# Attention and mixture-of-experts kernel: earlier value requests, other PSUM banks for two transposes, a last tile in halves

## The chip, the cores and the metric

The kernel runs on one core of a Trainium2 chip. The metric is the device time of one execution in microseconds; lower is better. Six executions of the kernel before took 402.0 to 403.68 us, with a median of 403.0 us.

## The reference

The first half is attention: 4 batches, 8 heads, 768 positions, 64 elements for each head. Heads 0, 2 and 6 ("retrieval") see every earlier key; the other five ("streaming") see the first 4 keys and a window of 64. The second half sends the 3072 rows of 512 elements through four experts, each with two layers, and adds their outputs with given weights:

```python
mask = np.where(retr[0, :, 0, 0, None, None], full_mask, stream_mask)
scores = np.where(mask[None, :, :, :], scale * q @ k.T, -1000000000.0)
a = softmax(scores); attn_out = a @ v
x = attn_out.transpose(0, 2, 1, 3).reshape(B * S, H * D)
p = domain_probs / (domain_probs.sum(-1, keepdims=True) + 1e-09)
for e in range(E):                       # E = 4
    h = np.maximum(x @ w1[e], 0.0)       # 512 -> 1024
    out += p[:, e:e + 1] * (h @ w2[e])   # 1024 -> 512
```

## The kernel before

**Groups.** The 3072 rows are cut into G = 8 groups of 384 (half a batch each). For a group, `attention` makes xT, the group's attention output transposed: four column tiles ct of 128 rows, each holding two heads. `moe_group` then runs the four experts over it. Groups overlap: while TensorE (PE) does the experts of group g, single steps of the attention of group g + 1 are put between its matmuls, by a written budget of time (`tick`, `att_ns`). Only group 0 has nothing to run beside: its attention comes first, alone. The order on every engine is the order in which the program is written; nothing is rescheduled.

**Group 0's attention** (`first`). Queries and keys of batch 0 come as float32 through the queues of SP and ACT, and TensorE transposes them (L495). For each head, `scores` multiplies (L596, L608), ACT takes the exponential into es (L614), and `values` multiplies es by the values: L644 for retrieval heads (tiles vR), L708 for streaming heads (tiles vS). Retrieval heads are divided on DVE (L657, L661, L664) into x_pair or x_one, which TensorE transposes (L685) and DVE copies to xT (L689). Streaming heads get a logarithm and an exponential on ACT (L726, L736) and a product on DVE (L731). Here and there `warm_up` (L387) puts matmuls on zeros between them, whose results nobody reads. The order at the end is: scores of head 7 together with values of head 6, values of head 5, the transposes of heads 2 and 6, values of head 7.

**Requests on POOL.** The values of all heads, the weights (converted to float16 on the way) and all later inputs are requested by POOL, one after another, in one queue (L268 and L274 values, L299 first-layer weights w1sb in two halves per expert, L305 second-layer weights w2sb). At the start the order is: values of head 0, the masks, values of heads 2, 1, 3, 4, then w1 of expert 0, values of heads 5, 6, 7, w2 of expert 0, clearing of tiles, keys and queries of group 1 (L211), w1 of expert 1, some of group 1's values, w2 of expert 1, and so on.

**Group 1's attention** still uses TensorE for the transposes of queries and keys (L498), four pairs hp of heads, queries and keys apart; DVE copies the results out: L507 queries, L514 and L530 keys (kS at L530). From group 2 on, DMA does these transposes.

**PSUM.** There are three pools: pA with four banks (`bank()`: scores, transposes of q and k, first layer of the experts), pV with two (values), pO with two (second layer, some values).

**The experts.** For each expert, the first layer makes eight tiles of 4 matmuls of 384 columns (L850, 32 in all), each read out by ACT (L863). The second layer makes three output tiles of 128 rows x 512 columns (L871, 8 matmuls each), which DVE scales and adds to acc (L883 for the first expert, L887 after). With the last expert, SP requests the store of each tile (L892).

Of the kernel before, what the change touches and what calls it, by code (L numbers as in the profile page):

```python
# [9 lines left out]
FP32 = mybir.dt.float32  # L10
FP16 = mybir.dt.float16
AF = mybir.ActivationFunctionType
ALU = mybir.AluOpType
# [4 lines left out]
def kernel(  # L18
# [33 lines left out]
    nc = tc.nc  # L52
    P = 128
    B, H, S, D = q.shape
    E, DM, F = moe_w1.shape
# [6 lines left out]
    FTP = F // P  # L62
    NTILE = N // P
    G = B * NCH
# [24 lines left out]
    pV = ctx.enter_context(tc.tile_pool(name="pV", bufs=1, space=bass.MemoryType.PSUM))  # L89
# [8 lines left out]
    def bank():  # L98
        return pA.tile([P, 512], FP32, name="pA", bufs=4)
# [3 lines left out]
    w2sb = pers.tile([P, E * FTP, DM], FP16, name="w2sb")  # L103
# [32 lines left out]
    p_sb = pers.tile([P, NTILE, E], FP32, name="p_sb")  # L136
# [19 lines left out]
    def own_v(h):  # L156
        return half(PLACE[h][1])
# [10 lines left out]
    def v_tiles(b, c, h):  # L168

        if RETR[h]:  # L170
            return vR[b % 2][:, 3 * c : 3 * c + 3, RH.index(h), :]
        if b:
            return windows(vSf, c)[:, :, SH.index(h), :]
        return vS[:, c, :, SH.index(h), :]
# [10 lines left out]
    def rows_of(x, b, h, c):  # L185
        return x[b, h, c * CH : (c + 1) * CH, :].rearrange("(j p) d -> p j d", p=P)

    def tiles_of(x, b, h, c):
        return x[b, h, c * CH : (c + 1) * CH, :].rearrange("(t r) d -> r t d", r=TK)

    def windows_of(x, b, h, c):

        assert b > 0
        first = ((b * H + h) * S + c * CH - WO) * D
        return bass.AP(x.tensor, x.offset + first, [[D, P], [WQ * D, WT], [1, D]])
# [68 lines left out]
    def load_v(b, c, heads):  # L264
        for h in heads:
            t = v_tiles(b, c, h)
            if RETR[h]:
                gp.dma_start(out=t[:, :, 0:D], in_=rows_of(v, b, h, c))  # L268
            elif b:
                gp.dma_start(  # L270
                    out=t[:, :, own_v(h)], in_=windows_of(v, b, h, c)
                )
            else:
                gp.dma_start(  # L274
                    out=t[R0:P, :, own_v(h)],
                    in_=tiles_of(v, b, h, c),
                )
# [72 lines left out]
    for h in range(H):  # L350
        if h == 2:
            nc.sync.dma_start(
                out=v_s32, in_=v[0, :, 0:NS, :].rearrange("h r d -> r h d")
            )
        nc.sync.dma_start(out=k32[:, :, h, :], in_=rows_of(k, 0, h, 0))
        if h == HP:
# [3 lines left out]
                    name=nc.get_next_instruction_name(),  # L360
# [6 lines left out]
        eng = nc.scalar if h < HP else nc.sync  # L367
        eng.dma_start(out=q32[:, :, h, :], in_=rows_of(q, 0, h, 0))
    nc.sync.dma_start(
        out=probs, in_=moe_domain_probs.rearrange("(t p) e -> p t e", p=P)  # L370
# [73 lines left out]

    mask_c(bC, 0.0, -60000.0)
    mask_s(bS[:, 0:2, :], 2, 0.0, -60000.0)
    load_v(0, 0, [2, 1, 3, 4])
    load_w1(0, 0, F)
    load_v(0, 0, [5, 6, 7])
    load_w2(0)  # L450
    zero(gp, kR[0][:, 1, :, :, :])
    zero(gp, kS[:, 1, :, :, :].rearrange("p t s x -> p s t x"))
# [24 lines left out]
    def mm_ns(cols):  # L477
        return cols / 2.4 + 2.5

    def attention(b, c):  # L480
        g = b * NCH + c
        i = b % 2
        first = g == 0
# [4 lines left out]

        def transposes(hp):
            for x, is_k in ((q32 if first else qt16, 0), (k32 if first else k16, 1)):  # L490
                ps = bank()
                for j in range(3):
                    o = ps[:, j * P : (j + 1) * P]
                    if first:
                        nc.tensor.transpose(o, x[:, j, 2 * hp : 2 * hp + 2, :], ident32)  # L495
                        continue
                    for u in range(2):
                        nc.tensor.matmul(  # L498
                            out=o[u * D : (u + 1) * D, :],
                            lhsT=x[:, 2 * hp + u, j, :],  # L500
                            rhs=ident16,
                            start=True,
                            stop=True,
                        )
                if not is_k:
                    op = nc.scalar.copy if first and hp < 2 else nc.vector.tensor_copy
                    op(out=rows_in_order(qTs[b, c][:, hp, :]), in_=cols(ps))  # L507
                    yield t_ns
                    continue
                for u in range(2):  # L510
                    h = 2 * hp + u
                    r = slice(u * D, (u + 1) * D)
                    if RETR[h]:
                        nc.vector.tensor_copy(  # L514
                            out=rows_in_order(
                                kR[i][r, c, RH.index(h), :, :].rearrange(
                                    "r t x -> r (t x)"
                                )
                            ),
                            in_=cols(ps[r, :]),  # L520
                        )
                        continue
                    n = SH.index(h)
                    x_in, x_out = ps[r, 0:CH], kS[r, c, :, n, R0:P]
                    if first:
                        x_in = x_in.rearrange("r (t x) -> r t x", x=TK)
                    else:
                        x_in = x_in.rearrange("r (j t p) -> r j t p", j=3, t=TC)
                        x_out = x_out.rearrange("r t (p j) -> r j t p", j=3)
                    nc.vector.tensor_copy(out=x_out, in_=x_in)  # L530
                    sinks = kS[r, c, :, n, 0:NS]
                    if c == 0:
                        src = ps[r, 0:NS]
                        op = nc.scalar.copy if hp < 2 else nc.vector.tensor_copy
                    else:
                        src, op = kS[r, 0, 0, n, 0:NS], nc.scalar.copy
                    src = src.rearrange("r (o x) -> r o x", o=1)
                    op(out=sinks, in_=src.to_broadcast([D, TC, NS]))
                yield 2 * t_ns
# [288 lines left out]
    def tick(ns):  # L828
        clock[0] += ns
        while behind and behind[0][0] <= clock[0]:  # L830
            behind.pop(0)[1]()


    def moe_group(g):
        nt0 = g * 3
        acc = {}
        for e in range(E):
            hs = moe.tile([P, FTP, CH], FP16, name="hs", tag="hs", bufs=2)


            ahead = 4 if g == 0 and e == 0 else 1
            for f0 in [0, *range(ahead, FTP)]:
                pss = {ft: bank() for ft in range(f0, f0 + (1 if f0 else ahead))}


                cts = (0, 2, 1, 3) if g == 0 else (2, 1, 3, 0)

                def layer1(ft, n):
                    ct = cts[n]
                    nc.tensor.matmul(  # L850
                        out=pss[ft][:, 0:CH],
                        lhsT=w1sb[:, e * DMP + ct, ft * P : (ft + 1) * P],
                        rhs=xT[g][:, ct, :],
                        start=(n == 0),
                        stop=(n == DMP - 1),
                    )

                for ft in pss:
                    for ct in range(DMP - 1):
                        layer1(ft, ct)  # L860
                for ft, ps in pss.items():
                    layer1(ft, DMP - 1)
                    nc.scalar.activation(  # L863
                        out=hs[:, ft, :], in_=ps[:, 0:CH], func=AF.Relu
                    )
                    yield DMP * mm_ns(CH), 0.6
            for j in range(3):
                nt = nt0 + j
                ps_o = pO.tile([P, DM], FP32, name="pO", bufs=2)
                for ft in range(FTP):  # L870
                    nc.tensor.matmul(  # L871
                        out=ps_o,
                        lhsT=hs[:, ft, j * P : (j + 1) * P],
                        rhs=w2sb[:, e * FTP + ft, :],
                        start=(ft == 0),
                        stop=(ft == FTP - 1),
                    )
                    if ft == FTP // 2 - 1:
                        yield FTP // 2 * mm_ns(DM), 1.4
                p_ap = p_sb[:, nt, e : e + 1]  # L880
                if e == 0:
                    acc[nt] = moe.tile([P, DM], FP32, name="acc", bufs=6)
                    nc.vector.tensor_scalar(  # L883
                        out=acc[nt], in0=ps_o, scalar1=p_ap, scalar2=None, op0=ALU.mult
                    )
                else:
                    nc.vector.scalar_tensor_tensor(  # L887
                        out=acc[nt], in0=ps_o, scalar=p_ap, in1=acc[nt],
                        op0=ALU.mult, op1=ALU.add,
                    )  # L890
                if e == E - 1:
                    nc.sync.dma_start(out=out[nt * P : (nt + 1) * P, :], in_=acc[nt])  # L892
                yield FTP // 2 * mm_ns(DM), 1.4
# [87 lines left out]
```

## Time and profile before

| | us |
|---|---|
| median of six runs (lowest, highest) | 403.0 (402.0, 403.68) |
| the profiled execution: its own time | 402.46 |
| the profiled execution: span, first to last instruction | 400.6 |
| TensorE busy | 391.2 (98% of the span) |
| ACT, DVE, POOL busy | 219.3, 155.9, 142.1 |
| attention of group 0, to the first matmul of L850 | 24.2 |
| from there to the last matmul | 372.4 |
| from the last matmul to the end of the span | 4.0 |

The 1.9 us between the span and the execution's own time lie outside the first and last instruction. Line numbers (L850) are those of the kernel before. In the timeline, a row is: start and length in us, engine, line, operation, output and inputs, shape, number of instructions, and in brackets the idle time of the engine before it and what ended that idle time. The rows of matmuls are modelled at their ends: a row's length holds about 0.17 us of the last matmul's way through the array.

### The profile page before, as it was taken

To read this page: it belongs to the slowest core of one execution; us is meant where nothing else is said; L and a number is where in the kernel's file an instruction comes from. 1 tells how busy PE (TensorE), PEld (TensorE's weight loads), DVE (VectorE), ACT (ScalarE), POOL (GpSimd) and SP (SyncE) were. 2 spreads that over 40 slices of the span, in tenths; PEclk is the share of its full clock that TensorE was granted. 3 is DMA by queue.
4 is the path that set the end of the run, shared out by engine and by line. 5 is a ranking of instruction groups with operands and counts; after the bars stand their busy time and mean duration, and the time that the engine had idled before them with its cause. 6 is when DMAs were issued, how large, how long until landed. Compare 5 with 4: busy or idle time off the path is not lost.

```text
span 400.6 us, 7112 instructions
## 1 busy us (share of the span) xinstructions
PE 391.2 (98%) x2821; PEld 222.1 (55%) x2821; DVE 155.9 (39%) x343; ACT 219.3 (55%) x468; POOL 142.1 (35%) x179
## 2 busy tenths in 40 slices
PE   8799999999999999999999999999999999999996
PEld 4664556555555555555555555555555555655552
DVE  7745556424342334334342233433443223422222
ACT  3752668535775545655664446845464456853331
POOL 8943776708908704910039301950000000000000
PEclk9989999999999999999999999999999999999999
DMA  9999999999999969990679949990482000020002
GB/s 168 158 201 200 199 203 153 127 181 134 127 190 147 119 121 119 131 114 2 118 99 161 89 77 136 100 163 12 71 128 81 3 11 0 11 79 2 0 2 79
DMA packets 165989, 42.23 MB, mean 105 GB/s; under 512 B 156380, under 2 KB 160836, under 8 KB 165956
## 3 DMA queue, kind: packets, MB, share of 16 engines
q0 software_dynamic: 102656, 20.98, 61.1%
q1 hardware_dynamic: 61700, 20.40, 26.1%
q10 hardware_dynamic: 1600, 0.39, 0.5%
q8 instruction: 22, 0.36, 0.4%
q14 instruction: 11, 0.09, 0.1%
HBM read 43.57 MB, written 6.29 MB: 124 GB/s over the span
## 4 chain that ended last, share of the span: by engine, by line
PE 90%; POOL 2%; DMA 2%; DVE 2%; ACT 2%; issue 1%; POOLq 0%; ACTq 0%
PE pA L850 41%; PE pO L871 40%; PE pA L596 5%; DMA vR<-in_v_dram 2%; PE pV L644 2%; PE pV L708 2%; PE pO L387 1%; POOL vS L274 1%; ACT es L614 1%; ACT hs L863 1%; DVE kS L530 1%; DVE acc L887 1%; POOL vR L268 0%; POOL bS L411 0%; POOL w1sb L299 0%
## 5 line engine op out<-in xcount | busy, mean ns | idle before, releaser
L850 PE MATMUL pA<-xT,w1sb 128*128 128x384 f16 x1024 | 185.9, 326 | 0.9 <-DVE kS L530 0.4
L871 PE MATMUL pO<-w2sb,hs 128*128 128x512 f16 x768 | 181.3, 379 | 0.0
L863 ACT ACTIVATE hs<-pA 128x384 f16<-128x384 f32 x256 | 122.0, 492 | 96.6 <-PE pA L850 91.3
L850 PEld LDWEIGHTS <-w1sb 128*128 128x128 f16 x1024 | 95.9, 98 | 60.4 <-issue 0.8
L871 PEld LDWEIGHTS <-hs 128*128 128x128 f16 x768 | 71.6, 98 | 73.2 <-ACT hs L863 0.7
L614 ACT ACTIVATE es<-pA 128x384 f16<-128x384 f32 (+2 forms) x122 | 60.6, 510 | 52.9 <-PE pA L596 50.4
L887 DVE SCALAR_TENSOR_TENSOR acc<-pO,p_sb,acc 128x512 f32<-128x512 f32 x72 | 54.0, 750 | 72.3 <-PE pO L871 72.0
L226 POOL DMA_DIRECT2D kSr<-in_k_dram x30 | 29.9, 1001 | 33.6 <-DMA kS<-kSr 22.5
L222 POOL DMA_DIRECT2D kRr<-in_k_dram x18 | 14.0, 778 | 73.0 <-DMA kR<-kRr 71.1
L731 DVE TENSOR_TENSOR xT<-pV,rc 64x384 f16<-64x384 f32 x37 | 20.5, 553 | 30.9 <-ACT rc L736 20.7
L270 POOL DMA_DIRECT2D vS<-in_v_dram x30 | 30.4, 1027 | 0.5 <-DMA q<-in_q_dram 0.5
L618 DVE TENSOR_TENSOR es<-es,mC 128x256 f16<-128x256 f16 (+1 forms) x42 | 10.9, 259 | 48.1 <-ACT es L614 47.2
L883 DVE TENSOR_SCALAR acc<-pO,p_sb 128x512 f32<-128x512 f32 x24 | 18.0, 751 | 27.9 <-PE pO L871 27.7
L726 ACT ACTIVATE rc<-pV,eps 64x384 f32<-64x384 f32 x37 | 21.3, 575 | 13.1 <-PE pV L708 12.5
L596 PE MATMUL pA<-qT,kR 128*128 128x384 f16 (+2 forms) x120 | 24.8, 278 | 0.7 <-ACT qT L507 0.4
L736 ACT ACTIVATE rc<-rc 64x384 f32<-64x384 f32 x38 | 19.8, 521 | 1.2
L268 POOL DMA_DIRECT2D vR<-in_v_dram x24 | 19.4, 809 | 1.8 <-DMA q<-in_q_dram 1.6
L644 PEld LDWEIGHTS <-es 128*128 128x128 f16 x252 | 13.3, 97 | 9.3 <-issue 2.1
L644 PE MATMUL pV<-vR,es 128*128 128x65 f16 x252 | 15.6, 193 | 2.1 <-DMA vR<-in_v_dram 1.9
L708 PEld LDWEIGHTS <-vS 128*128 128x128 f16 x255 | 13.8, 98 | 6.8 <-issue 0.5
L618 DVE TENSOR_TENSOR es<-es,mW 128x384 f16<-128x384 f16 x30 | 10.7, 358 | 17.1 <-ACT es L614 17.1
L596 PEld LDWEIGHTS <-kR 128*128 128x128 f16 x120 | 11.3, 98 | 10.2 <-DVE kR L514 0.7
(91 smaller groups left out, 185.1 us busy)
## 6 DMA issues: line engine op xcount, KB each, us to landing
out_dram<-acc SPq DMA_DIRECT2D x24, 256.0 KB
w1sb<-in_moe_w_dram POOLq DMA_DIRECT2D x8, 512.0 KB, 13.0
w2sb<-in_moe_w_dram POOLq DMA_DIRECT2D x4, 1024.0 KB, 15.5
kSr<-in_k_dram POOLq DMA_DIRECT2D x30, 112.0 KB, 3.9
vS<-in_v_dram POOLq DMA_DIRECT2D x30, 112.0 KB, 5.5
q<-in_q_dram POOLq DMA_DIRECT2D x18, 128.0 KB, 4.4
vR<-in_v_dram POOLq DMA_DIRECT2D x24, 48.0 KB, 4.6
kRr<-in_k_dram POOLq DMA_DIRECT2D x18, 48.0 KB, 4.2
```

The costliest lines, as they stand in the source:

```text
L226: gp.dma_start(out=kSr[:, :, SH.index(h), own(h)], in_=windows_of(k, b, h, c),)
L270: gp.dma_start(out=t[:, :, own_v(h)], in_=windows_of(v, b, h, c))
L596: nc.tensor.matmul(out=ps[:, o : o + nq], lhsT=key_tile(b, c, h, t), rhs=qTs[b, c][:, hp, q0 : q0 + nq], start=(n == 0 or not first), stop ...
L614: nc.scalar.activation(out=es[:, 0:cols], in_=ps[:, 0:cols], func=AF.Exp, scale=SC)
L618: nc.vector.tensor_tensor(out=es[:, o0:o1], in0=es[:, o0:o1], in1=m[:, mo : mo + o1 - o0], op=ALU.mult,)
L644: nc.tensor.matmul(out=ps[:, j, 0 : D + 1], lhsT=lhsT, rhs=vR[i][:, t, RH.index(h), 0 : D + 1], start=(n == 0), stop=(n == len(work) - 1), ...
L708: nc.tensor.matmul(out=ps[:, q0 : q0 + nq], lhsT=v_tile(b, c, h, t), rhs=es[:, o : o + nq], start=(n == 0), stop=(n == len(work) - 1), ski ...
L726: nc.scalar.activation(out=rc[r, :], in_=ps[o, 0:CH], func=AF.Ln, bias=eps[o, :])
L850: nc.tensor.matmul(out=pss[ft][:, 0:CH], lhsT=w1sb[:, e * DMP + ct, ft * P : (ft + 1) * P], rhs=xT[g][:, ct, :], start=(n == 0), stop=(n = ...
L863: nc.scalar.activation(out=hs[:, ft, :], in_=ps[:, 0:CH], func=AF.Relu)
L871: nc.tensor.matmul(out=ps_o, lhsT=hs[:, ft, j * P : (j + 1) * P], rhs=w2sb[:, e * FTP + ft, :], start=(ft == 0), stop=(ft == FTP - 1),)
L887: nc.vector.scalar_tensor_tensor(out=acc[nt], in0=ps_o, scalar=p_ap, in1=acc[nt], op0=ALU.mult, op1=ALU.add,)
```

## The change

There are three edits.

1. POOL's requests at the start: values of heads 6, 5 and 7 are requested directly after those of heads 2, 1, 3 and 4, and w1 of expert 0 after all of them. Before, w1 of expert 0 came first, and heads 5, 6, 7 after it. w2 of expert 0 follows in both.
2. In group 1, the transposes of the first two pairs of heads (four tiles: queries and keys of hp 0 and 1) take the two banks of pV in turn; those of hp 2 and 3 take banks of pA as before. Group 0 is not changed.
3. The last output tile of all (group 7, expert 3, third tile) is made by a new function `last_tile`: two halves of 256 columns, one after the other, each with 8 matmuls in a bank of pV, its own step on DVE, and its own store; the first is requested by SP, the second by ACT.

Nothing else moves: on each engine the other instructions stand in the same order.

```diff
-    load_v(0, 0, [2, 1, 3, 4])
+    load_v(0, 0, [2, 1, 3, 4, 6, 5, 7])
     load_w1(0, 0, F)
-    load_v(0, 0, [5, 6, 7])
     load_w2(0)
...
-                ps = bank()
+                if first or hp > 1:
+                    ps = bank()
+                else:
+                    ps = pV.tile([P, 512], FP32, name="pV", bufs=2)
...
+    def last_tile(e, nt, hs, acc):
+        for n, eng in enumerate((nc.sync, nc.scalar)):
+            cols = slice(n * DM // 2, (n + 1) * DM // 2)
+            ps = pV.tile([P, 512], FP32, name="pV", bufs=2)
+            for ft in range(FTP):
+                nc.tensor.matmul(
+                    out=ps[:, 0 : DM // 2],
+                    lhsT=hs[:, ft, 2 * P : 3 * P],
+                    rhs=w2sb[:, e * FTP + ft, cols],
+                    start=(ft == 0),
+                    stop=(ft == FTP - 1),
+                )
+            nc.vector.scalar_tensor_tensor(
+                out=acc[:, cols], in0=ps[:, 0 : DM // 2],
+                scalar=p_sb[:, nt, e : e + 1], in1=acc[:, cols],
+                op0=ALU.mult, op1=ALU.add,
+            )
+            eng.dma_start(out=out[nt * P : (nt + 1) * P, cols], in_=acc[:, cols])
...
+                if g == G - 1 and e == E - 1 and j == 2:
+                    last_tile(e, nt, hs, acc[nt])
+                    continue
```

## The prediction

> **What bounds the kernel now.** I read the page's chain that ended last, then the timeline of TensorE over the first 45 us and of all engines over the last ten, then POOL's timeline and the DMA view, because the first edit moves requests.
>
> ```profile
> span 400.6 us, 7112 instructions
> ...
> PE 90%; POOL 2%; DMA 2%; DVE 2%; ACT 2%; issue 1%; POOLq 0%; ACTq 0%
> ```
>
> TensorE is the chain, so only what makes it wait, slow down or end later counts. Its timeline shows where:
>
> ```profile
> 16.74 1.04 PE L387 MATMUL pV<-warm 128*128 128x256 f16 x8
> 19.72 0.34 PE L644 MATMUL pV<-vR,es 128*128 128x65 f16 x6 [1.94 <-DMA vR<-in_v_dram]
> 22.09 2.01 PE L387 MATMUL pO<-warm 128*128 128x256 f16 x10
> 24.19 5.64 PE L850 MATMUL pA<-xT,w1sb 128*128 128x384 f16 x32
> 35.62 1.47 PE L850 MATMUL pA<-xT,w1sb 128*128 128x384 f16 x8
> 37.78 2.12 PE L850 MATMUL pA<-xT,w1sb 128*128 128x384 f16 x12 [0.40 <-DVE kS L530]
> 42.09 1.03 PE L871 MATMUL pO<-w2sb,hs 128*128 128x512 f16 x4
> ```
>
> Edit 1 aims at the 1.94 us before 19.72 (head 6's values), edit 2 at the 0.40 us before 37.78, where a first-layer matmul needs a bank that DVE still copies from. The ten warm-ups at 22.09 take 0.2 us each, the eight at 16.74 0.11. The stretches say why (start:end, length, busy time of PE, PEld, DVE, ACT, POOL, then granted clock, DMA share, GB/s):
>
> ```profile
> 16.80:20.21 3.42, 1.47 (x19) 1.21 (x18) 1.23 (x3) 2.01 (x5) 3.42 (x6) 1.00 1.49 186
> 20.21:23.63 3.41, 3.41 (x22) 2.66 (x21) 1.58 (x5) 1.48 (x3) 2.54 (x4) 0.50 1.25 209
> ```
>
> After a stretch with TensorE busy 1.47 of 3.42 us, the clock was 0.50 for 3.41 us: the wait cost 1.94 us and then about 1.7.
>
> **Edit 1 on TensorE.** Six requests change places, none is added. Head 6's request starts at about 9.6, where w1 stood, not at 11.47. Head 4's values, directly ahead, landed at 14.7 (issue 8.92 + 5.8 in the DMA view), and w1's first half, ten times one head's bytes, at 16.7 (9.58 + 7.1). So head 6 lands between 14.7 and 16.7, nearer the former; TensorE asks at 17.6. That wait goes. What is late next:
>
> ```profile
> 18.17 0.69 ACT L614 ACTIVATE es<-pA 128x256 f16<-128x256 f32 x2
> 18.88 0.56 DVE L731 TENSOR_TENSOR xT<-pO,rc 64x384 f16<-64x384 f32 x1
> ```
>
> Head 6's third matmul needs the first of these exponentials, done at about 18.5; ACT has no gap from 15.2 on, so TensorE waits 0.9 us there. Then the transposes at L685 need x_pair: DVE ends L731 at 19.44, and L657, L661, L664 (0.16, 0.17, 0.36) bring it to 20.2, a second wait of about 0.4. From there at full clock: transposes 0.17, ten warm-ups 1.1, four matmuls of head 7 0.25. L850 begins at about 21.8 in place of 24.19: 2.4 us earlier. w1 of expert 0 now stands behind three value requests, but all four had landed by 20.0 (12.21 + 7.8), and the bytes are the same.
>
> **What comes of the 2.4 us.** Expert 1's first layer would begin at 35.62 - 2.4 = 33.2. Its weights are not there. In the DMA view, the request of its second half (issued at 19.71) and POOL's row that waits for its end:
>
> ```profile
> w1sb<-in_moe_w_dram POOLq DMA_DIRECT2D x1, 512.0 KB, 15.4
> ```
> ```profile
> 35.40 0.61 POOL L299 DMA_DIRECT2D w1sb<-in_moe_w_dram  x1 [1.65 <-DMA w1sb<-in_moe_w_dram]
> ```
>
> 19.71 + 15.4 = 35.1. From 20 to 35 us the DMA engines move 202 GB/s without a pause, and the edit changes the order at the head of the queue, not its bytes; POOL's requests from w2 of expert 0 (12.92) on keep their times, because the first that could wait for a displaced transfer starts at 20.3, after 20.0. So L850 starts at 35.16: **-0.46 us** stays of 2.4, and TensorE waits 2.0 us in a new place. Behind that wait stand only TensorE's own matmuls; the query and key transposes of pair 0 are ahead of it. SP's L292 copies, which waited for the values until 20.12, go earlier and have no hurry.
>
> **Edit 2.** From 35.62 to 42.09 there are 6.47 us, 0.40 of them the wait for DVE. L530 ended at 37.73; 2.4 us earlier is 35.3, before the second tile of L850 is done, so the wait would go by edit 1 alone, and with edit 2 the bank is not pA's anyway: **-0.40**, once. Price of the new banks: the queries of pair 1 need pair 0's copied out (L507 ended 35.27, now near 32.9), its keys L530; both are over before their transposes come. The next user of pV, values at 45.7, comes over 3 us after the last of these copies (41.85). Zero, and where DVE is late, 0.4 at most. The next weights: w2 of expert 1 lands at 21.81 + 19.1 = 40.9, TensorE comes at 42.09 - 0.86 = 41.2. Just clear. w1 of expert 2 (35.40 + 12.5 = 47.9) is needed at 49.3. From there on no DMA row ends a wait of TensorE, so the gain reaches the end.
>
> **Edit 3.** The end now:
>
> ```profile
> 393.97 3.79 SPq L892 DMA_DIRECT2D out_dram<-acc  x3
> 396.64 0.75 DVE L887 SCALAR_TENSOR_TENSOR acc<-pO,p_sb,acc 128x512 f32<-128x512 f32 x1 [0.98 <-PE pO L871]
> ```
>
> The waits have SP's L976 on the last store for 1.4 us. TensorE: 16 matmuls of 256 columns at 0.11 for 8 of 512 at 0.216 (5.18 us for 24), 0.02 us more. DVE on 256 columns: between 0.38 (half of 0.75) and 0.50 (0.36 for 192 columns at L664, 0.55 for 384 at L731, the difference put to 512 -> 256); I take 0.45, **-0.30**; the first half runs beside the second half's matmuls. The last store has half the bytes: 256 KB moved in 0.9 us (398.2 to 399.1, 291 GB/s), so **-0.45**, and zero if the first half is still under way; it starts 0.87 us earlier, enough for 128 KB. ACT's request is an addition: its four loads at the start took 0.55 each, SP's store 0.37 (no store from ACT is in the trace): **+0.2**. Sum -0.55, between -0.1 and -0.75.
>
> **Sum.** -0.46 - 0.40 - 0.55 = -1.4 us. Against the profiled execution (402.46) 401.05; that one lies 0.54 below the median of 403.0, so I forecast 403.0 - 1.4 = **401.6**.
>
> **Rivals.**
> - *The new wait halves the clock.* TensorE stands 2.0 us from 33.1 to 35.1, as long as the 1.94 us that was followed by half clock. If all of it falls in one stretch like 16.80:20.21, L850 at 35.16 loses 1.7 us (half of 3.41) with no slack to take it: 403.3, no measurable change (within 0.2%, 0.8 us, which is about what this kernel's runs can tell). If the wait is split between two stretches, each stays over 60% busy, which no row of before decides. An early half clock near 20 us would cost nothing, for it would only shorten the wait.
> - *Slower: the queue's head takes longer.* Heads 1, 3, 4 landed 1.4 us apart (11.9, 13.3, 14.7); heads 5, 6, 7, behind w1, 0.2 to 0.3 us apart. If the moved three also take 1.4 each, all that follows is up to 3.6 us later, w1 of expert 1 at 38.7, and the sum is +2.2: 405.2. It decides from a shift of 1.4 us on. Against it: the slow part is 10.0 to 12.5 us, at 88 GB/s; 12.5 to 14.5 has 149 and 17.5 to 20.0, where the three moved before, 180.
> - *The weights come earlier.* If expert 1's w1 did not bind (a shorter queue by 2 us), the whole 2.4 us would count: 399.6. Only the slow start of w1 (149 GB/s) speaks for part of it.
> - *Edits 2 and 3 do nothing*, because the bank wait goes by edit 1 and the last store by ACT costs what it saves: 402.1, inside the range.
>
> [...]
>
> **How the numbers follow.** Forecast 0.54, half clock 0.28, longer queue 0.10, earlier weights 0.08. The range leaves out the last two: 400.4 (tail at -0.75, weights 1 us early) to 403.6 (half clock, tail at -0.25). Faster than 402.2: forecast and earlier weights, 0.62. Within 0.2%: most of the half clock, 0.22. Slower than 403.8: the rest of it and the longer queue, 0.16. The forecast's own range is 400.8 to 402.2.
>
> **What would show it.** Right: no wait of L644 on vR; L850 first near 21.8; a wait of about 2 us on DMA w1sb at 35.1; no wait on L530; the last two DVE steps near 0.45 us. Wrong: TensorE reaching expert 1 without a wait, or a clock of 0.50 in the stretch after 35 us, or w1 landing after 36.

## The result, and the profile after

The changed kernel takes 404.56 us (median of 34 runs, 401.8 to 405.91) where the kernel before, run on the same chips, takes 402.88 (69 runs): a ratio of 1.0036, 95% interval 1.0027 to 1.0046. It is slower by 0.36%; the forecast was 401.6, and the range ended at 403.6.

Line numbers move: L644 is now L646, the first layer L850 is L872, the second layer L871 is L896, the transposes of group 1 L498 are L500, the keys' copy L530 is L532, and the halves of the last tile are L841 (PE), L848 (DVE) and L853 (stores). The profiled execution took 403.49, with a span of 401.4. Its page and then its timeline of TensorE, in the places shown of before:

```profile
span 401.4 us, 7130 instructions
...
PE 87%; POOL 5%; DMA 4%; ACT 2%; DVE 1%; issue 1%; POOLq 0%; ACTq 0%
```
```profile
17.73 0.22 PE L646 MATMUL pV<-vR,es 128*128 128x65 f16 x2
18.72 0.30 PE L646 MATMUL pV<-vR,es 128*128 128x65 f16 x4 [0.76 <-ACT es L616]
20.42 0.34 PE L687 MATMUL pV<-ident,x_pair 128*128 128x128 f16 x3 [0.28 <-DVE x_pair L666]
21.94 5.63 PE L872 MATMUL pA<-xT,w1sb 128*128 128x384 f16 x32
35.88 1.68 PE L872 MATMUL pA<-xT,w1sb 128*128 128x384 f16 x8 [2.44 <-DMA w1sb<-in_moe_w_dram]
37.95 3.31 PE L872 MATMUL pA<-xT,w1sb 128*128 128x384 f16 x12
43.44 1.03 PE L896 MATMUL pO<-w2sb,hs 128*128 128x512 f16 x4
```

The wait for head 6's values is gone, and expert 0 begins 2.25 us earlier. The wait that takes its place is 2.44 us long, and expert 1 begins at 35.88, later than the 35.62 of before. The twelve matmuls at 37.95 take 3.31 us where the same twelve took 2.12. The stretches around the wait (columns as in the prediction: busy time of PE, PEld, DVE, ACT, POOL, then granted clock, DMA share, GB/s) say why:

```profile
33.57:36.98 3.41, 1.10 (x7) 0.71 (x8) 1.86 (x3) 0.26 (x1) 1.61 (x3) 1.00 1.43 193
36.99:40.40 3.41, 3.41 (x17) 1.48 (x15) 0.80 (x1) 1.21 (x3) 0.99 (x2) 0.50 1.37 199
```

TensorE was busy 1.10 us of 3.41, and had half clock for the next 3.41. The delay against before at each place of the path:

| us from the span's start | before | predicted | after |
|---|---|---|---|
| expert 0 begins | 24.19 | 21.8 | 21.94 |
| w1 of expert 1 complete | 35.1 | 35.1 | 35.7 |
| expert 1's first layer begins | 35.62 | 35.16 | 35.88 |
| its second layer begins | 42.09 | 41.2 | 43.44 |
| from the last matmul to the end of the span | 4.0 | 3.45 | 3.46 |
| span | 400.6 | 399.2 | 401.4 |

The second layer of expert 1 begins 1.35 us late. No later wait of TensorE differs, so 1.35 less 0.55 at the end of the kernel is the 0.8 us of the span. This execution is one of the fast ones: its 403.49 lies 1.07 under the median.

The other runs differ from this one in how often the clock halves. One stretch of 3.41 us at half clock lowers the mean granted clock of a run by 0.004, so each run's mean tells the number of them (0.996 in this profile, which has one; the end of the span, where TensorE is done and its clock falls as well, to 0.50 at 400 us in the profile before, takes up to 0.002 more in the profiles):

| stretches at half clock | kernel before: runs, median | changed kernel: runs, median |
|---|---|---|
| none | 53, 402.13 | 3, 402.74 |
| one | 59, 402.92 | 18, 403.67 |
| two | 1, 404.3 | 13, 405.40 |

(Of before, the 113 runs beside e1 to e16.) In the kernel before, about half of the runs have one stretch, presumably the one at 20 us that the profile shows, and it costs only 0.8 us. The likely reason is that without it TensorE waits for w1 of expert 1 instead (0.9 us in the profile of e2, which has the old order and no half clock). In the changed kernel nearly every run has one, 13 of 34 have two, and a second one costs 1.7 us. But its three runs without any are no faster than those of before (402.74 against 402.13), though they hold edits 2 and 3: half clock is not the whole loss.

### The profile page after: what moved, and what is told of

Read it like the earlier page. It is cut to its first block, busy times and chain, and to the rows that moved or that the text cites. A ratio compares the mean times of both kernels' runs of the same rounds, so it can differ in the third digit from the quotient of the medians.

```text
span 401.4 us, 7130 instructions
## 1 busy us (share of the span) xinstructions
PE 391.2 (97%) x2829; PEld 222.2 (55%) x2829; DVE 156.4 (39%) x344; ACT 219.5 (55%) x468; POOL 142.2 (35%) x179
## 4 chain that ended last, share of the span: by engine, by line
PE 87%; POOL 5%; DMA 4%; ACT 2%; DVE 1%; issue 1%; POOLq 0%; ACTq 0%
PE pA L872 40%; PE pO L896 38%; PE pA L598 5%; DMA w1sb<-in_moe_w_dram 4%; PE pV L646 2%; PE pV L710 2%; POOL vS L274 1%; ACT es L616 1%; POOL vR L268 1%; ACT hs L885 0%; POOL w1sb L299 0%; POOL vS L325 0%; PE pV L841 0%; DVE kS L532 0%; POOL bS L411 0%
## 5 line engine op out<-in xcount | busy, mean ns | idle before, releaser
L872 PE MATMUL pA<-xT,w1sb 128*128 128x384 f16 x1024 | 187.3, 327 | 2.9 <-DMA w1sb<-in_moe_w_dram 2.4
L896 PE MATMUL pO<-w2sb,hs 128*128 128x512 f16 x760 | 179.5, 379 | 0.0
L872 PEld LDWEIGHTS <-w1sb 128*128 128x128 f16 x1024 | 96.3, 98 | 63.3 <-issue 4.8
L896 PEld LDWEIGHTS <-hs 128*128 128x128 f16 x760 | 70.8, 98 | 72.2 <-ACT hs L885 0.7
L646 PEld LDWEIGHTS <-es 128*128 128x128 f16 x252 | 13.4, 97 | 8.1 <-ACT es L616 1.1
L646 PE MATMUL pV<-vR,es 128*128 128x65 f16 x252 | 15.8, 193 | 0.9 <-ACT es L616 0.8
```

What stands on the lines that cost most here:

```text
L646: nc.tensor.matmul(out=ps[:, j, 0 : D + 1], lhsT=lhsT, rhs=vR[i][:, t, RH.index(h), 0 : D + 1], start=(n == 0), stop=(n == len(work) - 1), ...
L872: nc.tensor.matmul(out=pss[ft][:, 0:CH], lhsT=w1sb[:, e * DMP + ct, ft * P : (ft + 1) * P], rhs=xT[g][:, ct, :], start=(n == 0), stop=(n = ...
L896: nc.tensor.matmul(out=ps_o, lhsT=hs[:, ft, j * P : (j + 1) * P], rhs=w2sb[:, e * FTP + ft, :], start=(ft == 0), stop=(ft == FTP - 1),)
```

## The experiments

### The three edits apart

e1 is the kernel before with edit 1 alone (the order of the requests); e2 has edits 2 and 3 with the old order.

> Edit 1 alone on the kernel before. Clock theory (TensorE waits about 2.4 us for expert 1's w1 and one or two stretches of 3.41 us at half clock follow, 1.7 us each): as the changed kernel without the gain of its tail, 404.6 + 0.55 = 405.1, a wait of 2 to 2.5 us on DMA w1sb near 35 us, clock 0.50 after it. Stream theory (the value requests ahead of w1 make every later transfer 0.6 to 1.3 us late, and TensorE follows the queue, whatever the clock): also slower than before, 403.5 to 404.2, with w2 of expert 1 or w1 of expert 2 ending waits. Other-edits theory (the pV banks or the last tile cost the time): 402.9 or less.

> Edits 2 and 3 with the requests in the order of before. Clock and stream theories: 402.9 - 0.55 (tail) - 0 to 0.4 (wait on DVE before 37.8) = 401.9 to 402.4, no wait on DMA w1sb, the early wait on vR and the early half clock as before. Other-edits theory: 404 or more.

e1: 405.8 us against 402.75, ratio 1.0076 (1.0048 to 1.0103). e2: 402.3, ratio 0.9996 (0.9974 to 1.0019). The loss is edit 1's; the other two edits give at most a small gain. The profile of e1 has no half clock (1.00 from 7.01 to 51.38 us), and its execution took 402.72; its other six runs, 404.0 to 407.5, have one or two such stretches.

### Filling the wait

e3 puts matmuls on zeros into the new wait, so that TensorE is not idle; e4 puts group 1's transposes there.

```diff
+                if g == 0 and e == 1 and f0 == 0:
+                    warm_up(pss[0], 18, 256)
```
```diff
-            while done < (spent - begin) / (end - begin) * att_ns:
+            ahead_ns = 1300.0 if g == 0 and spent >= 0.99 * UNIT else 0.0
+            while done < (spent - begin) / (end - begin) * att_ns + ahead_ns:
```

> The changed kernel with 18 warm-up matmuls of 256 columns (0.11 us each, 2.0 us) ahead of expert 1's first layer, into the bank that the layer's first tile then overwrites. Clock theory: TensorE is busy while it waits, the clock stays at 1.00 after 35 us, and the time falls from 404.6 by 1.4 stretches of 1.7 us to about 402.1. Stream theory: the weights land when they land, 404.6 unchanged (404.2 to 405).

> The changed kernel with group 1's steps drawn 1300 ns earlier in the written budget from the end of expert 0 on, so that the transposes of queries and keys of pair 1 stand ahead of expert 1's first layer, in the wait, and later steps move up as well. Clock theory: 0.8 us of useful work in the wait, its idle part cut from 2.4 us in one piece to pieces of at most 1.6; half clock in fewer runs: 401.5 to 403.2. Stream theory: only the 0.8 us, 403.8.

e3: 405.08, ratio 1.0058 (1.0038 to 1.0079). Ten of its twelve runs have no half clock (a mean of 0.999 or 1.000), and they are no faster: 402.86 to 405.65. So something else was late too. Lines of its profile, three of TensorE and one of SP, show it, and below them SP's line in the kernel before:

```profile
32.64 0.36 PE L500 MATMUL pV<-ident,q 128*64 128x128 f16 x6 [1.44 <-DMA q<-in_q_dram]
...
37.24 1.46 PE L872 MATMUL pA<-xT,w1sb 128*128 128x384 f16 x8 [0.92 <-DMA w1sb<-in_moe_w_dram]
...
124.95 0.81 PE L872 MATMUL pA<-xT,w1sb 128*128 128x384 f16 x4 [0.76 <-DMA xT<-x_pair]
```
```profile
121.04 1.21 SPq L672 DMA_TRANSPOSE xT<-x_pair  x1
```
```profile
117.02 1.21 SPq L670 DMA_TRANSPOSE xT<-x_pair  x1
```

The queries of group 1 come later than in any profile of the old order (below). w1 of expert 1 is complete only at 37.1, 1.4 us later than in the profile after, so that TensorE still waits for it when its fill is done. And 90 us further on, the first layer of group 2 waits for the transpose of x_pair. SP issues that transpose at 121.04, behind its row of transposes for group 3; in the kernel before it issued it at 117.02.

e4: 404.5, ratio 1.0048 (1.0031 to 1.0065). Only 0.24 us of the wait for w1 is left, but in its place stands a wait of TensorE for a bank of pV, and the clock still halves (0.50 from 35.40 to 38.81 us):

```profile
35.14 0.36 PE L500 MATMUL pV<-ident,k 128*64 128x128 f16 x6 [1.92 <-DVE kS L532]
```

The keys of pair 1 need the bank from which DVE still copies those of pair 0. The two banks of edit 2 cost nothing in the order as written, and 1.92 us as soon as the second pair follows directly on the first.

### The second bound: SP's row of transposes

e5 lets SP request group 2's x_pair transpose ahead of its row for group 3, by starting that row later; e6 is e5 with the fill of e3.

```diff
-            if to_transpose and spent > {0: 0.87}.get(g, 0.5) * E * UNIT:
+            if to_transpose and spent > {0: 0.87, 1: 0.60}.get(g, 0.5) * E * UNIT:
```

> The changed kernel with SP's transposes for group 3 (issued during group 1) put behind the transpose of x_pair of group 2, not ahead of it. Third theory (late transfers make SP's long row of transposes end late, and group 2's first layer then waits for x_pair, as 0.8 us of it showed at 125 us with the wait filled): 404.6 falls to about 403. Clock theory (only the wait for expert 1's w1 and its half clock): 404.3 to 404.9. Stream theory as the clock theory.

> The filled wait (18 warm-ups ahead of expert 1's first layer) and x_pair first, together on the changed kernel. If half clock and the wait for x_pair are the two places: 402 to 402.8. If lateness of the weights alone sets the time: 404.5 to 405, as the filled wait alone (405.1).

e5: 404.93, ratio 1.0061 (1.0038 to 1.0083), no gain. e6: 403.27, ratio 1.0014 (1.0001 to 1.0026), every run without half clock (a mean of 0.999 or 1.000). Each alone gives nothing and both together 1.3 us by the medians (0.9 by the ratios): the half clock and the late x_pair are two bounds side by side. The profiles of e3 and e6 fit this: expert 1 begins at 37.24 and 37.28, neither has half clock, and of the 0.97 us between them 0.76 is e3's wait for x_pair.

### Why the queue is late

What is left of the loss in e6 is the queue itself. In its profile (403.25, like the median) the clock is full (1.00 from 33 to 40 us) and expert 1 begins 2.1 us later than the 35.16 of the prediction; the median lies 1.7 us above the forecast.

```profile
37.28 1.46 PE L872 MATMUL pA<-xT,w1sb 128*128 128x384 f16 x8 [1.47 <-DMA w1sb<-in_moe_w_dram]
```

In every profile with the new order the queries of group 1 are later than in any with the old one. e7 takes away a suspect, the probabilities' pieces of 16 bytes at the queue's head (3083 packets, 0.05 MB, in queue q1 from 10.0 to 12.9 us of the profile after): it loads them in 24 rows and lets TensorE transpose them. e8 does the same in the old order, with edits 2 and 3 and x_pair early.

```diff
-        out=probs, in_=moe_domain_probs.rearrange("(t p) e -> p t e", p=P)
+        out=probs_raw.rearrange("t p e -> t (p e)"),
+        in_=moe_domain_probs.rearrange("(t p) e -> t (p e)", p=P),
```

> The changed kernel with the expert weights of the rows (probs) loaded as 24 rows of 2 KB and transposed by four small matmuls on TensorE, in place of 3072 pieces of 16 bytes, which share the DMA engines with the moved value requests from 10 to 12.9 us. Stream theory (the queue's head is slow there, and all later transfers with it): w1 of expert 1 lands 0.7 to 1.2 us earlier, near 34.8, and the time falls to 403.2 to 403.8. Clock theory: the wait is shorter by as much but still over 1 us, half clock in fewer runs: 403 to 404. No effect of the queue's head: 404.6.

> Requests in the order of before, with edits 2 and 3, probs in rows and x_pair first. All theories expect no new wait; with the transfers about 1 us ahead and the tail shorter: 401.2 to 402.0, under both kernels.

e7: 405.36, ratio 1.0067 (1.0047 to 1.0086); the last of the eight requests for values lands at 13.5, not at 14.6, and the queries of group 1 as late as in the changed kernel (32.1 against 31.3). That was not it. e8: 402.0, ratio 0.9993 (0.9970 to 1.0017), but 400.57 to 402.58 in its eight runs without half clock.

e9 adds 18 warm-ups ahead of head 6's values, to hold TensorE back; e10 moves head 6 alone ahead of w1; e11 is e8 with both of its waits filled (10 and 18 warm-ups); e12 is e10 with the fill and the early x_pair of e6.

```diff
-                warm_up(ps, {6: 8}.get(h, 0), 256)
+                warm_up(ps, {6: 26}.get(h, 0), 256)
```
```diff
-    load_v(0, 0, [2, 1, 3, 4, 6, 5, 7])
+    load_v(0, 0, [2, 1, 3, 4, 6])
     load_w1(0, 0, F)
+    load_v(0, 0, [5, 7])
```

> The changed kernel with 18 more warm-ups (1.9 us) ahead of the values of head 6, so that TensorE reaches expert 0 at about 24 us again while POOL's requests keep the new order. Theory A (the new order of the requests itself makes the queue late): w1 of expert 1 is still complete only at 35.6 to 36.4 us, the queries of group 1 at 31.2 or later, and the time is 402.7 to 403.7. Theory B (the queue is late because TensorE, DVE and ACT are earlier and their loads and copies meet it): w1 of expert 1 is complete at 35.1 again, queries by 30.5, and the time is 401.6 to 402.5, below the kernel before by edits 2 and 3.

> The changed kernel, but only head 6 is requested ahead of w1 of expert 0; heads 5 and 7 stand behind it again, between w1 and w2. Theory A1 (the small requests between w1 and w2 keep the queue full there): w1 of expert 1 complete at about 35.1 to 35.5, queries by 30.5, time 402.5 to 403.5, what is left being the half clock after the wait for w1. Theory A2 (what costs is requests put ahead of w1): a third of the lateness of the changed kernel stays, queries at 30.2 to 31 and w1 of expert 1 at 35.4 to 36, time 403.3 to 404.2. Theory B (earlier TensorE): the same as the changed kernel, 404.0 to 404.8.

> The old order of requests with edits 2 and 3, the probabilities loaded in rows, group 2's last transpose early (all as in e8), and both remaining waits of TensorE filled: 10 more warm-ups ahead of the values of head 6 and 18 ahead of the first layer of expert 1. Theory A: no stretch at half clock is left, and with the queue in its old order the time is 400.6 to 401.5 (e8 measured 402.0, and its profile, with one stretch at half clock, 403.4). Theory B (clock and order do not matter together; something else late ends the waits): 402 to 403.5.

> e10 with 18 warm-ups ahead of the first layer of expert 1 and with group 2's last transpose early, so e6 with only head 6 moved. Theory A1: 401.6 to 402.6, the queue late by little and no half clock. Theory A2: 402.4 to 403. Theory B: as e6, 403.3.

e9 (404.44, ratio 1.0050, 1.0031 to 1.0069) missed its aim: the warm-ups ran inside the waits for ACT and x_pair, and expert 0 began at 21.63 all the same. e10: 402.36, ratio 1.0010 (0.9983 to 1.0038), some 2 us less than the changed kernel by the medians, 1 by the ratios, for two requests put back. Expert 0 begins at 21.44, and the queue is in time (w1 of expert 1 at 34.6), so TensorE's being early does not by itself delay it. e11: 402.13, ratio 0.9995 (0.9981 to 1.0009), and e12: 402.67, ratio 1.0000 (0.9981 to 1.0020), have no half clock in any run and yet no gain: in the profiles TensorE began expert 1 at 36.48 and 35.96, after its fill, when w1 had been there since 35.6 and 35.2. A fill that overshoots costs what it was meant to save.

Heads 5 and 7 ahead of w1 do two things: no small request stands between w1 and w2 any more, and SP's copies of values (L292), which before had to wait for head 7, start at 17.4 us and not at 20. e13 delays the copies alone (a small DVE step they must wait for), e14 puts two small requests of group 1 between w1 and w2.

```diff
+        nc.vector.memset(vS[0:NS, c, :, 0, 0:1], 0.0)
         for t in range(TC):
             nc.sync.dma_start(
```
```diff
     load_w1(0, 0, F)
+    load_v(0, 1, [0, 2])
     load_w2(0)
...
-    load_v(0, 1, [0, 2])
```

> The changed kernel with SP's four copies (L292) made to wait for a small DVE step of group 1, so that they start after 20 us as in the kernel before. Theory C (the copies at 17.4 us meet the weights on the DMA engines and make the queue late): queries of group 1 by 30.5, w1 of expert 1 at 35.1 to 35.5, time 402.3 to 403.3. Theory A (what matters is that no small request stands between w1 and w2 of expert 0): queue and time as in the changed kernel, queries at 31.2 or later, 404.0 to 404.8.

> The changed kernel with two small requests that were further back (group 1's values of heads 0 and 2) moved between w1 and w2 of expert 0; SP's copies stay at 17.4 us. Their 256 KB are now ahead of keys, queries and w1 of expert 1 only in part, for they stood behind w1 of expert 1 before: that alone makes queries and w1 about 0.4 us later. Theory A: apart from these 0.4 us the queue is in time again, queries by 30.9, w1 of expert 1 at 35.5, time 402.5 to 403.8. Theory C: the queue is as late as in the changed kernel or by 0.4 us more, 404.3 to 405.3.

e13: 404.15, ratio 1.0032 (1.0015 to 1.0048); the copies went at 31.84, later than meant, and w1 of expert 1 was complete at 36.4. e14: 405.75, ratio 1.0071 (1.0050 to 1.0092), w1 at 37.5. Neither theory holds: e13 is as late without the early copies, which speaks against C, and e14 stayed late with small requests in between, which speaks against A. e14 is the weaker test: its two requests (48 KB each in the DMA view, so 96 KB, not the 256 of the expectation) kept POOL for 1.5 us, and what follows was requested later by as much. The 20 profiles of all kernels show where the queue loses time (GB/s of the DMA engines, and completion in us):

| order of requests | profiles | 14.5 to 17.5 us | 20 to 21 us | queries of group 1 | w1 of expert 1 |
|---|---|---|---|---|---|
| old | 7 | 197 to 208 | 200 to 209 | 29.5 to 30.6 | 35.1 to 36.2 |
| head 6 ahead of w1 | 3 | 197 to 209 | 202 to 210 | 30.0 to 31.8 | 34.6 to 36.0 |
| heads 6, 5, 7 ahead | 10 | 152 to 200 | 96 to 200 | 31.2 to 32.7 | 35.6 to 37.5 |

Most profiles of the new order lose time at the start of w1, and most where w1 of expert 0 gives way to w2. Neither place is shown to be the cause: e7 has 200 and 179 GB/s there, and its w1 of expert 1 is complete at 36.35 all the same. The ranges of the last column overlap; the middle values are 35.5 in the old order and 36.3 in the new one. By the times of their packets, the engines are not idle at the start of w1. The DMA view of one microsecond, 15 to 16 us, after and then before (packets, bytes, rate; the queue's packets, MB and share of 16 engines):

```profile
DMA packets 54, 0.11 MB, mean 111 GB/s; under 512 B 0, under 2 KB 0, under 8 KB 54
...
q0 software_dynamic: 54, 0.11, 100.7%
```
```profile
DMA packets 116, 0.21 MB, mean 207 GB/s; under 512 B 15, under 2 KB 15, under 8 KB 116
...
q0 software_dynamic: 116, 0.21, 112.0%
```

In both the packets fill the engines' time, but a packet takes 0.30 us after (1.007 x 16 us over 54) and 0.15 before (1.12 x 16 over 116, of which 15 are under 512 bytes). Why the queue is late when eight requests of values stand ahead of w1 (heads 0, 2, 1, 3, 4, 6, 5, 7) and not when five or six do, stays open.

### A shorter fill, and a version below both

e15 and e16 take 8 warm-ups (0.9 us) for the fill of expert 1: e15 with head 6 alone ahead (e12 otherwise), e16 in the old order (e8 otherwise). e17 and e18 take one of e16's other edits away: e17 the probabilities in rows, e18 the early x_pair.

> e12 with 8 warm-ups (0.9 us) ahead of the first layer of expert 1 in place of 18. In e10 the wait there was 1.6 us and the runs without half clock took 401.3; 18 warm-ups (2.1 us) overshot the landing of w1. If the half clock follows from the length of the wait alone, nearly every run is without it and the median is 401.2 to 401.8, below both kernels. If 0.9 us less wait is not enough to keep the clock, the runs split as in e10 and the median is 402 to 403.

> e8 (old order, edits 2 and 3, probabilities in rows, group 2's last transpose early) with 8 warm-ups ahead of the first layer of expert 1; the wait for head 6 is left as it is. Runs of e8 without half clock took 400.6 to 401.6, of 0.3 us more than e10's best. If the fill keeps the clock, the median is 400.9 to 401.6; if the wait for head 6 alone halves it, that half clock falls before the wait for w1 and costs nothing, so the same; if the fill costs its own length, 401.8 to 402.4.

> e16 without the probabilities in rows: old order, edits 2 and 3, group 2's x_pair transpose early, 8 warm-ups ahead of expert 1's first layer. Theory P (the late x_pair is what limits): 401.0 to 401.4, as e16. Theory R (the probabilities' 16-byte pieces slow the queue's head in the old order): 402.0 to 402.5.

> e16 with the x_pair transpose in its old place, behind the row of transposes: old order, edits 2 and 3, probabilities in rows, 8 warm-ups. Theory P: 402.0 to 402.5. Theory R: 401.0 to 401.4. If both runs lie near 401.6, each edit brings part.

| | us | ratio to before | runs without half clock |
|---|---|---|---|
| e15 | 402.44 | 0.9984 (0.9969 to 0.9999) | 10 of 11 |
| e16 | 401.07 | 0.9967 (0.9952 to 0.9982) | 11 of 12 |
| e17 | 402.69 | 0.9985 (0.9970 to 1.0000) | 5 of 12 |
| e18 | 402.83 | 1.0000 (0.9975 to 1.0025) | 9 of 12 |

The short fill keeps the clock in nearly every run of e15 and e16. e15's median missed its bound by 0.6 us: the runs of e10 without half clock may have been those in which w1 came early (34.6 in its profile, 36.0 in e15's), which was not shown. e16 is below both kernels, by 0.33% of before. Its profiled execution is its slowest (403.63): there w1 of expert 1 came at 36.2, and w2 of expert 2 ended a wait of 1.06 us. Neither theory on its parts won: without the one or the other the median is 402.7 to 402.8, so the early x_pair and the probabilities in rows seem to count only together; the kernel with neither and the short fill was not run. Half clock is not all of it: the runs without it have medians of 401.0 (e16), 401.9 (e17) and 402.4 (e18).

## Why the prediction was wrong

**The first steps held.** L646 no longer waits for vR; the waits behind it were put at 0.9 and 0.4 us and are 0.76 and 0.28; expert 0 was put at 21.8 and begins at 21.94. Two later steps failed, each worth more than a microsecond: full clock after the new wait, and the transfers' times taken as unchanged.

**The first step that failed is the forecast's choice at the new wait.** The prediction had a row of before that showed half clock after a wait of 1.94 us, priced the same after the new wait of 2.0 us at 1.7 us, and gave it 0.28; the forecast, full clock, got 0.54. Of 34 runs 31 have at least one such stretch. The price of a stretch was right (1.5 us in the profile, 1.7 for a second stretch); the chance was not, and a second stretch was not thought of. The prediction left the decision to where the wait falls between two stretches, "which no row of before decides". It also held that a split wait leaves each stretch over 60% busy, which is so only where no part is over 1.36 us. The experiments' rows decide it. Here are the stretches of 3.41 us that hold the new wait, and the next ones, in the profiles of e15, e10 and e9:

```profile
33.95:37.35 3.40, 1.73 (x13) 0.92 (x11) 1.53 (x3) 0.37 (x1) 1.72 (x3) 1.00 1.33 202
37.37:40.77 3.40, 3.40 (x30) 1.89 (x29) 1.30 (x2) 2.27 (x6) 0.86 (x2) 1.00 1.53 195
```
```profile
31.26:34.67 3.41, 1.80 (x18) 0.71 (x17) 2.81 (x5) 0.00 (x0) 0.65 (x1) 1.00 1.38 195
34.68:38.09 3.41, 3.40 (x25) 1.96 (x26) 1.22 (x2) 1.68 (x4) 1.95 (x3) 1.00 1.24 208
```
```profile
32.05:35.46 3.41, 1.23 (x10) 0.40 (x9) 3.05 (x4) 0.00 (x0) 1.26 (x2) 1.00 1.39 192
35.47:38.88 3.41, 2.41 (x8) 1.05 (x8) 0.00 (x0) 0.49 (x1) 1.95 (x3) 0.50 1.27 207
38.89:42.29 3.40, 3.40 (x16) 1.63 (x16) 0.80 (x1) 0.98 (x2) 0.00 (x0) 0.50 1.56 189
```

Busy for 0.51 and 0.53 of a stretch, TensorE kept its clock; busy for 0.36, it lost it, and since the end of the wait lay in the next stretch (busy 0.71, at half clock), it lost it for two. In 20 profiles every stretch at full clock with a busy share of 0.51 or more was followed by full clock, and every one of 0.48 or less by half clock, but for one (e1: 0.41). The stretches lie on a grid of 3.41 us whose place in the span differs from profile to profile (its first full-clock stretch begins between 3.9 and 7.1 us; in the profiles before and after the half clock comes 13.66 and 30.72 us later, 4 and 9 stretches). A wait of 2 us within one stretch leaves at most 0.41 of it. An estimate from these numbers: the clock stays full if the wait is split so that neither part is over about 1.7 us (half of 3.41, between the 0.48 and the 0.51). With 2.0 us the border must then fall into the middle 1.4 us, 0.41 of the places on the grid, and with 2.4 us into the middle 1.0, 0.29; measured are 3 runs of 34. Of the six profiles with a wait of 2.7 to 3.2 us, four had two stretches (e5, e7, e9, e14), one had one (e13) and one none (e1); after 2.4 us there was one (after, e8). So the likeliest case was half clock, not full clock, and the split a way out for the lucky phase.

**The second step that failed: the queue's times were taken as unchanged.** The prediction held that six requests in another order carry the same bytes and that all had landed by 20.0, so that w1 of expert 1 is complete at 35.1 as before. POOL's requests did keep their times (that of w1's second half 19.70, before 19.71); the transfers did not. The DMA view after has w1 of expert 0 and of expert 1, second halves, issued at 12.28 and 19.70:

```profile
w1sb<-in_moe_w_dram POOLq DMA_DIRECT2D x1, 512.0 KB, 8.8
...
w1sb<-in_moe_w_dram POOLq DMA_DIRECT2D x1, 512.0 KB, 16.0
```

That is 21.1 for the first and 35.7 for the second, 0.6 later than predicted; over the ten profiles of the new order 0.5 to 2.4 later, 1.2 in the middle. This step alone puts the forecast out of reach: e6, at full clock in every run, takes 403.27, with w1 of expert 1 complete at 37.1 in its profile. Why the order makes the transfers late stays open. The rival of the longer queue had the right sign and a sixth of its price in the profiled run (0.6 of its 3.6 us), for a reason that it did not name. How far the three values land apart did not decide it: head 4 landed at 14.0 and heads 6, 5 and 7 within 0.7 us of it, and the loss came after them, in the weights and what follows.

**"From there on no DMA row ends a wait"** holds in the profile after, but with little to spare: the x_pair transpose, issued at 118.44, comes 1.4 us later than before, and in e3 it is the next bound. The prediction followed POOL's queue and not SP's. In e15 and e16 later weights end waits as well (w2 of expert 1 0.48 us, w2 of expert 2 1.06).

**Edits 2 and 3 held.** No wait stands on L532, which was put at -0.40; none stands there in e1 either, without edit 2, as the prediction had it. The tail was put at -0.55 and is -0.55:

```profile
396.07 1.91 PE L841 MATMUL pV<-w2sb,hs 128*128 128x256 f16 x16
...
397.15 0.48 DVE L848 SCALAR_TENSOR_TENSOR acc<-pV,p_sb,acc 128x256 f32<-128x256 f32 x1
...
398.02 0.48 DVE L848 SCALAR_TENSOR_TENSOR acc<-pV,p_sb,acc 128x256 f32<-128x256 f32 x1 [0.39 <-PE pV L841]
398.54 0.37 ACTq L853 DMA_DIRECT2D out_dram<-acc  x1
```

DVE's half was put at 0.45 and takes 0.48. ACT's request takes 0.37, as long as SP's of before, where 0.2 more had been added; what follows the request became only 0.3 us shorter, where the store had been put at 0.45. The two errors cancel, so the exact sum is luck.

**Sum, as it came in the profile:** expert 1 begins 0.26 later instead of 0.46 earlier (the queue: +0.72), the half clock adds 1.5, the bank wait gives 0.40, the tail 0.55: +0.8 in the span. The median run is 1.07 us slower than this one. The lateness of the other profiles (1.2 in the middle) and the second stretch in 13 of 34 runs (1.7) are of a size to explain that; no median run was traced.

## What to carry to other kernels

Here a wait of 1.94 us was taken away ahead of a queue that was already full (202 GB/s from 20 to 35 us of the profile before); the time went to the next transfer that ended late (a wait of 2.44 us for w1 of expert 1), and the new wait stood where nothing could absorb what followed it. Do not take the queue's times as unchanged because the bytes are: w1 of expert 1 came 0.5 to 2.4 us later in the ten profiles of the new order. Price the clock with the wait: in these profiles a wait that left TensorE busy for less than about half of a stretch of 3.41 us cost, with one exception, that wait and up to 1.7 us more, or 3.4 with a second stretch; eight matmuls on zeros (0.9 us) that ended before the data landed avoided that in 21 of 23 runs (e15, e16), and 18 of them cost what they overshot (0.9 and 0.8 us in the profiles of e11 and e12). Where one bound is removed and nothing changes, look for a second that ends at the same time, on another queue, before the first is called harmless.

## What the runs showed of the hardware

- In the 20 profiles the clock went with TensorE's busy share in the stretch of 3.41 us before: after 0.51 to 0.57 it stayed at 1.00 (e15, e10, e6), after 0.25 to 0.48 it was 0.50 (ten profiles), with one exception at 0.41 (e1). Once halved, a busy share of 0.44 to 0.71 kept it halved (e14, e5, e7, e9), and 0.89 or more brought it back (e17, before, after).
- The place of these stretches differs between the 20 profiles by up to 3.2 us (the first at full clock begins at 3.9 to 7.1 us), and the number of stretches at half clock between runs of one program: none, one or two in the 34 runs of the changed kernel, whose medians lie 2.7 us apart of the 4 us between its fastest and slowest run.
- The rate at the start of the weights was 152 to 200 GB/s with eight requests for values in front (48 KB each), 197 to 209 with five or six. In the profile after, packets of 2 KB took 0.30 us each at 15 to 16 us; before, the mean of 116 packets, 15 of them small, was 0.15.
